# Attention, gated MLP and mixture on one core: products with V four tiles behind the scores, four buffers of transposed exponentials and two of split ones

## The chip, the cores and the metric

The program runs on one core of a Trainium2 chip. A core has five engines that each take their instructions in order from a queue of their own: TensorE (PE, with its weight loads shown apart as PEld), VectorE (DVE), ScalarE (ACT), GpSimd (POOL) and SyncE (SP), which here only issues transfers. They meet through semaphores. The metric is the device time of one execution in microseconds; what is compared is the median of several executions.

## The reference, cut to what matters

```
scores = scale * q @ k.T                      # 4 batches, 8 heads, 576 keys, head 64
thresh = max(scores, -1) - tau
scores = where(scores >= thresh, scores, -1e9)
attn   = exp(scores - max(scores));  attn /= sum(attn)
x      = (attn @ v), heads side by side       # 2304 tokens x 512
xn     = x / rms(x) * g
x      = (silu(xn @ w_gate) * (xn @ w_val)) @ w_out
P      = balance(exp(x @ w_gate2))            # 8 rounds of row and column sums
out    = sum over 8 experts e of P[:, e] * (relu(x @ w1[e]) @ w2[e])
```

The change lies in the attention, in the step from the exponentials to their product with V.

## The kernel before, in words

The program has two stages on one TensorE. In the first, attention and the gated MLP run together. In the second, the mixture of experts runs alone; nothing of the change touches it.

Attention goes by 144 tiles, one for 128 queries of one head (32 a batch), or for 64 remaining queries of two heads (4 a batch). For a tile, `att_tile` issues the following. TensorE computes the scores S (L282, four matmuls of 288 columns, eight in a tile of remaining queries) into one of two PSUM buffers. VectorE takes their maximum (L292). ScalarE makes two small tables (L293, L297) and the exponential e (L296), which VectorE masks by the threshold while it sums it (L298); this is the last reading of S, and it frees the PSUM buffer for the tile after the next. ScalarE then rounds e to 16 bits into the first half of a tile `hl` (L303), and GpSimd writes what the rounding left out into the second half (L304, L305). SyncE issues one transfer that transposes `hl` into a tile `eT` (L307). TensorE at last multiplies `eT` with V (L330, `att_values`, 14 matmuls of 64 columns, 28 in a tile of remaining queries).

Since that chain is long, the product with V of a tile isn't issued with its scores. A list `waiting` holds the tiles whose products are still open, and when it holds more than `LAG` of them, the oldest is issued behind the scores of the present tile, `with tc.issue_after(last.ins)`: on TensorE's queue it can't stand ahead of them. `LAG` also sets at which tile of a batch V is rounded (`prepare`, the calls of `prep_v`), and how many products follow after the last scores.

`hl` has three buffers and `eT` three. A buffer of `hl` can be written again when the transposing transfer of its earlier tile has landed; one of `eT` when the products of its earlier tile are done. The waits stand on ScalarE's queue (ahead of L303) and on SyncE's (ahead of L307).

When a group of tiles has ended (`end_main`, `end_rem`), its rows are scaled (L376, L395), normalised and sent transposed to the MLP. The gated MLP takes two groups at a time: `mlp_in` (L530 on TensorE, L538 to L545 on ScalarE, VectorE and GpSimd), then `mlp_out` (L561). Its weights are decoded and scaled during the first tiles.

The order on each queue is fixed before the program runs, by a planner with modelled durations: of what its plan has ready on an engine it takes the attention first (`attention_order`), and the MLP where attention isn't ready. On the chip an instruction that comes to the head of its queue too early holds everything behind it.

Of the kernel before, what the change touches and what calls it, by code (L numbers as in the profile page):

```python
# [8 lines left out]
F16 = mybir.dt.float16  # L9
# [10 lines left out]
def kernel(  # L20
# [25 lines left out]
    B, H, S, D = q.shape  # L46
# [3 lines left out]
    P = 128  # L50
# [92 lines left out]
    pa = pa_cm.__enter__()  # L143
# [91 lines left out]
    def prep_v(st, a):  # L235

        b, s_v = st["b"], st["s_v"]
        vs = pa.tile([P, 2, H2, NW, D], F16, tag="vs", name=f"vs{b}_{a}", bufs=2)
        st["vs"].append(vs)
        r = st["raw_v"][:, a * H2 : (a + 1) * H2]  # L240
        A.activation(vs[:, 0], r, AF.Copy, scale=s_v[:, 0:1])
        V.scalar_tensor_tensor(
            vs[:, 1].rearrange("p h c d -> p (h c d)"),
            r.rearrange("p h c d -> p (h c d)"),
            s_v[:, 0:1],
            vs[:, 0].rearrange("p h c d -> p (h c d)"),
            ALU.mult,
            ALU.subtract,
        )

    def prep_q(st, c):
        b = st["b"]
        qs = pa.tile([P, H, 2, D], F16, tag="ks", name=f"qs{b}_{c}", bufs=2)
        qr, s_q = st["raw_q"], st["s_q"]
        A.activation(qs[:, :, 0, :], qr[:, :, c, :], AF.Copy, scale=s_q[:, c : c + 1])
        V.scalar_tensor_tensor(
            qs[:, :, 1, :], qr[:, :, c, :], s_q[:, c : c + 1], qs[:, :, 0, :], ALU.mult, ALU.subtract
        )
        qT = pa.tile([P, H, P], F16, tag="qT", name=f"qT{b}_{c}", bufs=2)
        qX = pa.tile([P, H, P], F16, tag="qX", name=f"qX{b}_{c}", bufs=2)  # L260
        nc.sync.dma_start_transpose(out=qT, in_=qs.rearrange("p h l d -> p (h l d)"))
        nc.sync.dma_start(out=qX[0:64], in_=qT[64:128])
        nc.sync.dma_start(out=qX[64:128], in_=qT[0:64])
        st["q", c] = (qT, qX)
# [1 line left out]
    HS = S // 2  # L266

    waiting = []
    LAG = 3

    def att_tile(st, c, heads, slot, group):

        kT = st["kT"]
        qT, qX = st["q", c]
        nm = f"{st['b']}_{c}_{heads[0]}"
        sums = group["sums"]
        sp = psa.tile([P, 2, 512], F32, tag="S", name=f"S{nm}", bufs=2)
        rows = P // len(heads)
        for qq, first in ((qT, True), (qX, False)):
            for i, h in enumerate(heads):  # L280
                for j in range(2):
                    last = T.matmul(  # L282
                        sp[i * rows : (i + 1) * rows, j, 0:HS],
                        lhsT=qq[:, h, 0:rows],
                        rhs=kT[h // H2][:, h % H2, j * HS : (j + 1) * HS],
                        start=first,
                        stop=not first,
                    )
        sv = sp[:, :, 0:HS]
        nt = pa.tile([P, 3], F32, tag="nt", name=f"nt{nm}", bufs=4)  # L290
        mx = nt[:, 2:3]
        V.tensor_reduce(mx, sv, AX.XY, ALU.max)  # L292
        A.activation(nt[:, 0:1], mx, AF.Copy, scale=st["wt"][:, c : c + 1])  # L293
        e = pa.tile([P, S], F32, tag="e", name=f"e{nm}", bufs=3)
        ev = e.rearrange("p (a n) -> p a n", a=2)
        A.activation(ev, sv, AF.Exp, bias=nt[:, 0:1], scale=st["c2"][:, c : c + 1])  # L296
        A.activation(nt[:, 1:2], mx, AF.Identity, bias=st["bt"][:, c : c + 1])  # L297
        V.scalar_tensor_tensor(  # L298
            ev, sv, nt[:, 1:2], ev, ALU.is_ge, ALU.mult, accum_out=sums[:, slot : slot + 1]
        )  # L300

        hl = pa.tile([P, 2 * S], F16, tag="hl", name=f"hl{nm}", bufs=3)
        A.activation(hl[:, 0:S], e, AF.Copy)  # L303
        G.tensor_tensor(hl[:, S + REM :], e[:, 0 : NCH * P], hl[:, 0 : NCH * P], ALU.subtract)  # L304
        G.tensor_tensor(hl[:, S : S + REM], e[:, NCH * P :], hl[:, NCH * P : S], ALU.subtract)  # L305
        eT = pa.tile([P, 2 * S // P, P], F16, tag="eT", name=f"eT{nm}", bufs=3)
        nc.sync.dma_start_transpose(out=eT, in_=hl)  # L307
        waiting.append((st, heads, slot, group, eT))
        if len(waiting) > LAG:

            with tc.issue_after(last.ins):
                att_values(*waiting.pop(0))

    def att_values(st, heads, slot, group, eT):
        if slot == 0:
            group["pv"] = psa.tile([P, H * D], F32, tag="pv", name=f"pv{group['n']}", bufs=1)
        rows = P // len(heads)
        for i, h in enumerate(heads):
            vs, hh = st["vs"][h // H2], h % H2
            o = group["pv"][i * rows : (i + 1) * rows, slot * D : (slot + 1) * D]  # L320
            cols = slice(i * rows, (i + 1) * rows)
            mm = []
            for cc in range(NCH):
                mm.append((eT[:, cc, cols], vs[:, 0, hh, cc, :]))
                mm.append((eT[:, cc, cols], vs[:, 1, hh, cc, :]))
                mm.append((eT[:, NW + cc, cols], vs[:, 0, hh, cc, :]))
            mm.append((eT[:, NCH, cols], vs[:, 0, hh, NCH, :]))
            mm.append((eT[:, NCH, cols], vs[:, 1, hh, NCH, :]))
            for n, (a, r) in enumerate(mm):
                T.matmul(o, lhsT=a, rhs=r, start=n == 0, stop=n == len(mm) - 1)  # L330
        if slot == group["last"]:
            ended.append(group)
# [296 lines left out]
    def prepare(b, o):  # L629

        st = states[b]
        if o < NCH * H and o % H == 1:
            prep_q(st, o // H + 1)
        if b > 0 and o in (LAG - 3, LAG - 1):
            prep_v(st, (o - LAG + 3) // 2)
        if b + 1 == B:
# [33 lines left out]

    for t in range(len(row) + LAG):
        before = tc.cur_priority
        with attention_order():
            if t < len(row):
                b, c, heads, n, g = row[t]
                if n == 0:
                    g["sums"] = pa.tile([P, H], F32, tag="sums", name=f"sums{g['n']}", bufs=2)
                att_tile(states[b], c, heads, n, g)
                prepare(b, t % SLOTS)
            else:  # L680
                att_values(*waiting.pop(0))
            done = list(ended)
            ended.clear()
            for g in done:
                (end_main if g["c"] < NCH else end_rem)(g)
        first += tc.cur_priority - before
        for g in done:
            i = g["i"]
            if i == 1:
                for gi in range(NG):  # L690
                    prep_group(gi)
                first = tc.cur_priority
                tT = mlp_in(0)
                prep_out()
                mlp_out(0, tT)
            elif i is not None and i % 2 == 1 and i < len(tiles) - 1:
                mlp_out(i // 2, mlp_in(i // 2))
# [283 lines left out]
```

## Time and profile before

| what | us |
|---|---|
| median of 3 runs | 2198.3 (2198.22 to 2200.58) |
| the profiled execution | 2195.02 |
| its span, first to last instruction | 2193.2 |
| TensorE busy | 2032.0 |
| VectorE busy | 1490.2 |

The profile shows one execution. Engine shares are averages over both stages; the first tile of attention starts at about 39 us, the last product with V at 623 us, and the gated MLP ends at about 720 us. In the rows below, a gap before an instruction is given with what ended it: `[2.09 <-DMA eT<-hl]` means that the engine was idle for 2.09 us until the transfer from `hl` to `eT` had landed. `x14` counts instructions.

### The profile page before, as it was taken

To read this page: it belongs to the slowest core of one execution; us is meant where nothing else is said; L and a number is where in the kernel's file an instruction comes from. 1 tells how busy PE (TensorE), PEld (TensorE's weight loads), DVE (VectorE), ACT (ScalarE), POOL (GpSimd) and SP (SyncE) were. 2 spreads that over 40 slices of the span, in tenths; PEclk is the share of its full clock that TensorE was granted. 3 is DMA by queue.
4 is the path that set the end of the run, shared out by engine and by line. 5 is a ranking of instruction groups with operands and counts; after the bars stand their busy time and mean duration, and the time that the engine had idled before them with its cause. 6 is when DMAs were issued, how large, how long until landed. Compare 5 with 4: busy or idle time off the path is not lost.

```text
span 2193.2 us, 35334 instructions
## 1 busy us (share of the span) xinstructions
PE 2032.0 (93%) x13872; PEld 1194.7 (54%) x13872; DVE 1490.2 (68%) x3026; ACT 870.9 (40%) x1774; POOL 471.0 (21%) x572
## 2 busy tenths in 40 slices
PE   1358789899999999999999999999999999999999
PEld 0236667666876755545555555555555555555554
DVE  6999677777744287865775765766757757666554
ACT  6878778877843243311221221222212212222111
POOL 1347556665743231000000000000000000000000
PEclk9859999999999999999999999999999999999999
DMA  9895879867826051000100100100001001000001
GB/s 267 207 201 100 169 145 174 159 144 115 147 55 142 18 144 40 29 30 1 39 20 20 39 20 20 39 20 20 20 20 39 20 20 39 20 20 1 1 28 60
DMA packets 321879, 154.10 MB, mean 70 GB/s; under 512 B 278960, under 2 KB 292400, under 8 KB 321712
## 3 DMA queue, kind: packets, MB, share of 16 engines
q1 hardware_dynamic: 321120, 151.82, 30.4%
q8 instruction: 108, 1.77, 0.3%
q14 instruction: 59, 0.48, 0.1%
q0 software_dynamic: 64, 0.00, 0.0%
q10 hardware_dynamic: 528, 0.02, 0.0%
HBM read 68.18 MB, written 12.98 MB: 37 GB/s over the span
## 4 chain that ended last, share of the span: by engine, by line
PE 70%; DVE 2%; DMA 1%; SPq 1%; POOL 0%; issue 0%; ACT 0%; DVEq 0%; ACTq 0%
PE y L906 33%; PE h L860 28%; PE gv L530 5%; PE x L561 2%; PE pv L330 1%; DMA w1r<-in_moe_w_dram 1%; SPq L762 0%; PE S L282 0%; DMA x2T<-x2d 0%; DVE w L714 0%; DMA w2r<-in_moe_w_dram 0%; DMA eT<-hl 0%; PE logits L804 0%; DVE w1m L725 0%; POOL xh L601 0%
## 5 line engine op out<-in xcount | busy, mean ns | idle before, releaser
L860 PE MATMUL h<-x2T,w 128*128 128x384 f16 x4032 | 703.8, 326 | 9.9 <-DMA x2T<-x2d 3.9
L860 PEld LDWEIGHTS <-w 128*128 128x128 f16 x4032 | 394.1, 98 | 300.0 <-issue 14.2
L921 DVE SCALAR_TENSOR_TENSOR acc<-y,coef,acc 128x512 f32<-128x512 f32 x270 | 198.1, 746 | 283.0 <-PE y L906 282.9
L730 POOL TENSOR_TENSOR w1s<-w1r 128x512 f32<-128x512 f32 x16 | 20.3, 1271 | 1060.3 <-DMA w1r<-in_moe_w_dram 1006.3
L304 POOL TENSOR_TENSOR hl<-e,hl 128x512 f16<-128x512 f32 x144 | 172.8, 1200 | 228.2 <-ACT hl L303 146.2
L906 PE MATMUL y<-w,hD 128*128 128x512 f16 x864 | 219.9, 379 | 0.0
L906 PE MATMUL y<-w,hA 128*128 128x512 f16 x864 | 210.6, 379 | 0.9 <-DVE acc L921 0.6
L906 PE MATMUL y<-w,hC 128*128 128x512 f16 x864 | 210.0, 379 | 0.2 <-ACT acc L917 0.2
L906 PE MATMUL y<-w,hB 128*128 128x512 f16 x864 | 210.0, 379 | 0.0
L848 ACT ACTIVATE hA<-u 128x384 f16<-128x384 f32 x96 | 50.2, 522 | 341.1 <-DVE u L876 320.9
L848 ACT ACTIVATE hB<-u 128x384 f16<-128x384 f32 x96 | 50.2, 523 | 312.1 <-DVE u L880 311.2
L530 PE MATMUL gv<-xnT,wg 128*128 128x256 f16 x1296 | 167.8, 278 | 4.5 <-DVE u L540 3.0
L530 PE MATMUL gv<-xnT,wv 128*128 128x256 f16 x1296 | 167.5, 275 | 0.0
L330 PE MATMUL pv<-vs,eT 128*128 128x64 f16 (+1 forms) x2240 | 103.1, 201 | 50.3 <-DMA eT<-hl 47.3
L561 PE MATMUL x<-wo,tT 128*128 128x512 f16 x648 | 144.4, 379 | 1.0 <-DVE u L540 0.9
L906 PEld LDWEIGHTS <-hB 128*128 128x128 f16 x864 | 84.5, 98 | 101.9
L530 PEld LDWEIGHTS <-wg 128*128 128x128 f16 x1296 | 126.5, 100 | 24.0 <-issue 4.1
L298 DVE SCALAR_TENSOR_TENSOR e<-S,nt,e 128x576 f32<-128x576 f32 x144 | 116.3, 809 | 32.0 <-ACT e L296 31.5
L906 PEld LDWEIGHTS <-hD 128*128 128x128 f16 x864 | 84.6, 98 | 95.4
L530 PEld LDWEIGHTS <-wv 128*128 128x128 f16 x1296 | 126.4, 99 | 16.0 <-issue 0.2
L906 PEld LDWEIGHTS <-hC 128*128 128x128 f16 x864 | 84.7, 98 | 91.9 <-issue 0.3
L330 PEld LDWEIGHTS <-eT 128*128 128x128 f16 (+1 forms) x2240 | 91.0, 106 | 79.1 <-DMA eT<-hl 62.1
(244 smaller groups left out, 2852.1 us busy)
## 6 DMA issues: line engine op xcount, KB each, us to landing
w1r<-in_moe_w_dram SPq DMA_DIRECT2D x16, 1024.0 KB, 4.9
w2r<-in_moe_w_dram SPq DMA_DIRECT2D x16, 1024.0 KB, 5.3
wgatew<-in_moe_w_gate_dram SPq DMA_DIRECT2D x12, 512.0 KB, 6.0
wo<-in_moe_w_out_dram SPq DMA_DIRECT2D x12, 512.0 KB, 4.2
wvalw<-in_moe_w_val_dram SPq DMA_DIRECT2D x12, 512.0 KB, 4.5
x2d<-xs SPq DMA_DIRECT2D x24, 256.0 KB, 2.5
qX<-qT SPq DMA_DIRECT2D x40, 128.0 KB, 3.5
raw_k<-in_k_dram SPq DMA_DIRECT2D x4, 1024.0 KB, 6.2
```

The source lines that it names most:

```text
L298: V.scalar_tensor_tensor(ev, sv, nt[:, 1:2], ev, ALU.is_ge, ALU.mult, accum_out=sums[:, slot : slot + 1])
L304: G.tensor_tensor(hl[:, S + REM :], e[:, 0 : NCH * P], hl[:, 0 : NCH * P], ALU.subtract)
L330: T.matmul(o, lhsT=a, rhs=r, start=n == 0, stop=n == len(mm) - 1)
L530: T.matmul(gv[:, a, :], lhsT=w[:, l, kk, f * P : (f + 1) * P], rhs=xt[:, r * KD + kk, :], start=n == 0, stop=n == 3 * KD - 1,)
L561: T.matmul(ps, lhsT=tT[f][:, l, o : o + P], rhs=wo[:, f, r, :], start=n == 0, stop=n == 3 * KF - 1,)
L730: G.tensor_tensor(sm[:, 0], a21, a22, ALU.add)
L848: A.activation(t[:, 0, :], src, AF.Relu)
L860: T.matmul(ps, lhsT=w[:, a, l, kk, f * P : (f + 1) * P], rhs=xb[:, b * 4 + r * 2 + kk, :], start=n == 0, stop=n == 5,)
L906: T.matmul(ps, lhsT=hs[a][f][:, l, jj * P : (jj + 1) * P], rhs=w2[:, r, f, :], start=n == 0, stop=n == 3 * KH - 1,)
L921: V.scalar_tensor_tensor(acc[i], ps, coef[h][:, i : i + 1], acc[i], ALU.mult, ALU.add)
```

## The change

`LAG` becomes 4 in place of 3, so that a tile's products with V stand behind the scores of the fourth tile after it. `hl` has two buffers in place of three and `eT` four in place of three; a tile of either takes 2304 bytes a partition, so the memory stays the same. Through `LAG`, the two calls of `prep_v` for batches 1 to 3 move from tiles 0 and 2 of a batch to tiles 1 and 3, and four products instead of three follow the last scores.

```diff
     waiting = []
-    LAG = 3
+    LAG = 4
 
     def att_tile(st, c, heads, slot, group):
...
-        hl = pa.tile([P, 2 * S], F16, tag="hl", name=f"hl{nm}", bufs=3)
+        hl = pa.tile([P, 2 * S], F16, tag="hl", name=f"hl{nm}", bufs=2)
         A.activation(hl[:, 0:S], e, AF.Copy)
         G.tensor_tensor(hl[:, S + REM :], e[:, 0 : NCH * P], hl[:, 0 : NCH * P], ALU.subtract)
         G.tensor_tensor(hl[:, S : S + REM], e[:, NCH * P :], hl[:, NCH * P : S], ALU.subtract)
-        eT = pa.tile([P, 2 * S // P, P], F16, tag="eT", name=f"eT{nm}", bufs=3)
+        eT = pa.tile([P, 2 * S // P, P], F16, tag="eT", name=f"eT{nm}", bufs=4)
         nc.sync.dma_start_transpose(out=eT, in_=hl)
         waiting.append((st, heads, slot, group, eT))
         if len(waiting) > LAG:
```

## Rows read from the trace of the kernel before

**Rows 1.** The page: busy time, share of the span and instructions of each engine.
```profile
PE 2032.0 (93%) x13872; PEld 1194.7 (54%) x13872; DVE 1490.2 (68%) x3026; ACT 870.9 (40%) x1774; POOL 471.0 (21%) x572
```

**Rows 2.** Busy time by stretch: PE, PEld, DVE, ACT, POOL; then granted clock, DMA.
```profile
60.00:160.00 100.00, 44.95 (x370) 27.26 (x370) 95.03 (x197) 81.76 (x169) 40.21 (x42) 0.69 0.86 201
160.00:520.00 360.00, 320.65 (x3547) 244.48 (x3545) 276.88 (x658) 283.62 (x660) 222.19 (x293) 0.97 0.78 147
520.00:625.00 105.00, 103.98 (x1179) 77.39 (x1178) 73.75 (x176) 78.01 (x179) 71.30 (x99) 1.00 0.74 132
625.00:725.00 100.00, 95.93 (x709) 69.53 (x708) 34.67 (x80) 30.28 (x63) 30.09 (x38) 0.98 0.39 88
```

**Rows 3.** Waits of PE, 160 to 625 us: total, times, longest.
```profile
PE pv L330 <- DMA eT<-hl: 22.7, 21, 3.8
PE S L282 <- DVE e L298: 5.2, 5, 1.9
```

**Rows 4.** Waits of PE, 60 to 160 us.
```profile
PE pv L330 <- DMA eT<-hl: 24.6, 8, 4.7
PE S L282 <- DVE e L298: 19.1, 7, 6.9
```

**Rows 5.** Timeline of PE at two of the waits: start, us, instruction, idle before.
```profile
241.98 0.93 PE L330 MATMUL pv<-vs,eT 128*128 128x64 f16 x14 [3.76 <-DMA eT<-hl]
...
322.27 0.26 PE L330 MATMUL pv<-vs,eT 128*128 128x64 f16 x3 [2.27 <-DMA eT<-hl]
322.37 0.41 PE L282 MATMUL S<-kT,qT 128*128 128x288 f16 x2
322.62 0.41 PE L282 MATMUL S<-kT,qX 128*128 128x288 f16 x2
322.86 0.48 PE L330 MATMUL pv<-vs,eT 128*128 128x64 f16 x11
```

**Rows 6.** PE behind those waits: busy, granted clock, DMA share, GB/s.
```profile
242.00:246.00 4.00, 4.00 (x33) 0.59 0.94 247
324.00:332.00 8.00, 7.33 (x59) 0.59 0.51 97
```

**Rows 7.** Tile hl, 160 to 625 us: ns min/median/max, first and last start.
```profile
L303 ACT ACTIVATE hl<-e x122: 665/674/686, 161.8 to 614.1; 128x576 f16<-128x576 f32 x122
L304 POOL TENSOR_TENSOR hl<-e,hl x122: 1149/1158/1692, 162.6 to 614.9; 128x512 f16<-128x512 f32 x122
L305 POOL TENSOR_TENSOR hl<-e,hl x122: 297/308/1556, 163.7 to 616.0; 128x64 f16<-128x64 f32 x122
...
  DMA eT<-hl: 1.3, 2
...
DMA to landing us min/median/max: 3.2/3.4/7.1
```

**Rows 8.** The chain of waits, 546.9 to 558.5 us: start, us, what.
```profile
549.71 0.69 ACT hl L303
...
551.90 0.70 POOL x2t L589
...
552.83 4.97 DMA eT<-hl
```

**Rows 9.** Timeline of ACT in the same stretch.
```profile
555.77 0.67 ACT L303 ACTIVATE hl<-e 128x576 f16<-128x576 f32 x1
556.34 0.46 ACT L538 ACTIVATE u<-gv,g 128x256 f32<-128x256 f32 x1
556.70 0.29 ACT L293 ACTIVATE nt<-nt,wt 128x1 f32<-128x1 f32 x1
```

**Rows 10.** Timelines of DVE and PE: a mask, and the scores two tiles on.
```profile
561.07 0.82 DVE L298 SCALAR_TENSOR_TENSOR e<-S,nt,e 128x576 f32<-128x576 f32 x1 [0.89 <-ACT e L296]
...
563.21 0.41 PE L282 MATMUL S<-kT,qT 128*128 128x288 f16 x2
```

**Rows 11.** Tile hl, 520 to 625 us.
```profile
L303 ACT ACTIVATE hl<-e x31: 667/677/686, 522.5 to 614.1; 128x576 f16<-128x576 f32 x31
```

## The prediction

> **What bounds the kernel now.** I read the page first: TensorE is busy for 93% of the span, VectorE for 68% [rows 1]. The end is set by TensorE's work plus its idle time, so I asked for the engines by stretch, to see where that idle time lies. Up to 160 us VectorE is the bound (95.0 of 100 us busy, TensorE 45.0). From 160 to 520 us TensorE is busy for 320.7 of 360 us, so it idles 39 us; from 520 to 625 us it idles 1 us; behind that there is only MLP work until the mixture [rows 2]. The stretch that a change of the attention can win from is thus 160 to 520 us, and its price list is TensorE's waits: 22.7 us in 21 waits of L330 for the transfer from `hl` to `eT`, and 5.2 us in five waits of L282 for the mask of L298 [rows 3]. So the products with V do come too early on TensorE's queue; more than half of what can be won there is this wait. Before 160 us the same wait takes 24.6 us and the scores' wait 19.1 us [rows 4], while VectorE has hardly a pause.
>
> **The change, part by part.** *Products one tile later.* After 160 us, 122 tiles start between 161.8 and 614.1 us [rows 7], one every 452.3/121 = 3.74 us. A product that stands one tile later has 3.74 us more on average, as long as the longest wait (3.8 us). But tiles come in pairs on TensorE. At 241.98 us MLP matmuls follow the late product, and the whole 3.76 us can go; at 322.27 us the next scores follow at once, and the product is only pushed behind them (two rows of 0.41 us that overlap by 0.16, so 0.5 us up to the next group) and behind the products of the tile before (0.4 us): 0.9 us of cover [rows 5]. Of the 21 waits eleven are over 0.9 us. One is that at 241.98 us; I give 0.9 us to each of the other ten, though some have MLP matmuls between as well, and that leaves 5.8 us of their 14.8. Gain: 22.7 - 5.8, about 17 us. From both sides: 0 (all moves into another wait) and 22.7 us.
>
> *The clock.* Behind two of the waits the granted clock falls to a mean of 0.59, that is, to 1.2 of 2.4 GHz for most of these stretches: 4 us busy behind the wait of 3.76 us, and 7.33 us busy behind that of 2.27 us and a wait for scores [rows 6]. At full clock this work would be shorter by up to 0.41 x 11.3 = 4.6 us. The second stretch has its other wait left, so I take half: 2.3 us, between 0 and 4.6.
>
> *Two buffers of split exponentials.* This is the price. A buffer of `hl` is held from the start of L303 until the transfer has landed. At medians: ScalarE 0.67, GpSimd 1.16 + 0.31, landing 3.4 = 5.5 us [rows 7], and more where something stands in between: in the chain, L303 starts at 549.71, an MLP subtraction of GpSimd stands ahead of the issue, and the transfer lands at 557.80, 8.1 us later [rows 8]. L303 of two tiles on started at 555.77 [rows 9]; with two buffers it would wait for 2.0 us. With three, ScalarE waited for such a landing for 1.3 us in all [rows 7]. I set each of the 122 L303 against the landing of two tiles before (issue plus its own time to landing): 59 of them start before it, by 73.3 us in all, 4.8 us at most. Behind the waiting L303 on ScalarE's queue stand the Tanh of the MLP (L538) and the tables of the next tile (L293) [rows 9], behind those the exponential, the mask, and the scores of two tiles on. ScalarE is busy for 361.6 of 465 us between 160 and 625 (283.6 and 78.0 [rows 2]), so 73 us would fit into its idle 103 but use most of it. What reaches TensorE is what the scores have no slack for. At 563.21 us scores start 1.3 us after the mask of two tiles before has ended (561.07 + 0.82) [rows 10]; paired like this the median over the 122 tiles is 1.56 us. Of the 59 late starts 18 are late by more than 1.5 us, by 18.4 us beyond it. Part of this falls on moments where TensorE has products with V ready ahead of the scores, which now are a tile older. I take a little over half, 10 us. The ends are 0 (the planner spreads the tiles where it runs out of buffers) and 27 us (rival 1). I take a value nearer to the row-by-row sum than to either.
>
> The Trainium skill, on its page "Trainium Kernel Development and Optimization", section "Best Practices", asks for two buffers where a transfer is to overlap with compute. By that rule the third buffer was spare, the price would be 0, and the sum would come to some 2179 us. The trace bears that out only while a hold stays under two tiles' time; the hold of 8.1 us does not. I go by the rows.
>
> *Four buffers of transposed ones.* The issue of L307 now waits for the products of four tiles before, which themselves come one tile later: the same distance. Zero, with the same distance hiding it. *prep_v and the last products.* V of a batch is rounded one tile later and needed one tile later: zero. Its ScalarE and VectorE work meets other neighbours, which I bound by plus or minus 1 us. The last products end one tile later at most, with some 96 us of MLP matmuls left after 625 us [rows 2] that need none of them at first: zero; without that cover it would be one tile, 3.7 us.
>
> *Before 160 us.* VectorE idles 5 us of 100 [rows 2], so no more than 5 us can be won although TensorE's two waits there sum to 43.7 us [rows 4]. The missing buffer can cost as much. I take 0, between -5 and +5.
>
> The sum: -17 - 2.3 + 10 = -9 us on the profiled execution's own 2195.0 (its span of 2193.2 and 1.8 us around it), 2186 us. The median of the runs shown lies 3.3 us above that execution, which gives 2189 us.
>
> **The rivals.** *1. Two buffers set the pace: slower.* Held as long as in this trace (mean of the 122 pairs of start and landing: 6.96 us), two buffers pass one tile in 3.48 us. The mean pace is 3.74 us, but from 520 to 625 us the 31 tiles come every (614.1 - 522.5)/30 = 3.05 us [rows 11], and their mean hold of 6.68 us allows 3.34. TensorE is full there [rows 2], so 30 x 0.29 = 8.7 us would be new idle time; with the whole 18.4 us of the late starts it is 27 us, against a gain of 17: +10, 2208 us. It decides from the point at which holds exceed twice the planned tile time. For it: tiles come in pairs, holds of 8 us occur, and 18 of 122 tiles would start later than the scores have slack for. Against it: unhindered, the hold is 5.5 us, and the planner also sees that there are two buffers and can put MLP matmuls between.
>
> *2. One wait for another: no change.* Products stop waiting, and the scores of L282 wait instead for masks that come late: 17 us against 17 to 20, 2196 to 2200 us. For it: L282's wait already exists in five places. Against it: the slack of 1.56 us at the median.
>
> *3. The price is hidden: clearly faster.* All waits of L330 go, both stretches of low clock with them, and up to 3 of the 5 us before 160 us: 22.7 + 4.6 + 3 = 30 us, 2168 us. For it: ScalarE's idle 103 us. Against it: ten of the eleven long waits may have only 0.9 us of cover.
>
> That the change doesn't move the products is hardly possible, since `issue_after` ties them to the later scores; that the planner's order of everything else comes out different, with waits of its own of a few microseconds either way, is in all ranges.
>
> **How the numbers follow.** The forecast (a gain of 5 to 17 us, so 2181 to 2193 around 2189) has a chance of 0.42, rival 1 0.25, rival 2 0.17, rival 3 0.16. The predicted time is the forecast's, 2189 us. A measurement of this kernel can tell about 0.2%, 4.4 us, from no change. The forecast lies beyond it nearly all through (0.39 of its 0.42), rival 3 wholly: faster 0.55. Rival 2 and the edges of the forecast and of rival 1 give the same: 0.20. The rest of rival 1 is slower: 0.25. The range reaches from 2166 us (rival 3 and 2 us) to 2212 (rival 1 and 4 us).
>
> **What would show it.** Right: the wait of L330 for `eT` between 160 and 625 us falls from 22.7 to some 6 us; ScalarE gets a wait of L303 for the transfer, from 1.3 to some tens of microseconds; L282's wait for L298 grows by about 10 us; TensorE's idle time between 160 and 520 us falls from 39 to about 30. Wrong: L303 hardly waits (the price was none), or TensorE idles from 520 to 625 us as well and L282's wait grows by 20 us or more (rival 1), or L330 still waits for 15 us or more, since the pairs of tiles give it no more time.

## The result, and the profile after

The changed kernel takes 2211.2 us at the median against 2198.3 us of the kernel before run beside it: ratio 1.0051 (95% interval 1.0039 to 1.0064), 12.9 us slower. (Here and below the microseconds are differences of medians. The ratio is formed over the runs otherwise than as the quotient of the two medians, which is 1.0059 here; it is given for its interval.) The forecast was 2189 us; the time is near that of rival 1, which had 2208.

The page of the kernel after, its span and its busy times (before: [rows 1]):

```profile
span 2210.5 us, 35361 instructions
PE 2038.1 (92%) x13872; PEld 1195.8 (54%) x13872; DVE 1496.6 (68%) x3026; ACT 870.5 (39%) x1774; POOL 471.6 (21%) x572
```

The span grew by 17.3 us (this profiled execution is 1.2 us above the median, that of before 3.3 below). TensorE has the same 13872 matmuls; it is busy 6.1 us longer, and so idle 11.2 us longer. The same stretches as in [rows 2], and the piece in which its clock differs most (busy time of PE, PEld, DVE, ACT, POOL, then granted clock and DMA):

```profile
60.00:160.00 100.00, 41.50 (x355) 26.23 (x354) 92.25 (x189) 79.50 (x162) 39.87 (x40) 0.64 0.84 195
160.00:520.00 360.00, 318.21 (x3416) 239.00 (x3416) 271.37 (x642) 274.55 (x640) 214.27 (x285) 0.96 0.78 144
520.00:625.00 105.00, 99.46 (x1084) 73.19 (x1082) 75.33 (x169) 77.09 (x179) 65.92 (x91) 1.00 0.70 125
...
160.00:240.00 80.00, 63.48 (x642) 47.29 (x642) 65.60 (x151) 55.85 (x135) 47.40 (x57) 0.87 0.64 122
```

Idle time of TensorE: 58.5 us from 60 to 160 (before 55.0), 41.8 from 160 to 520 (39.4), 5.5 from 520 to 625 (1.0). So the loss is in every stretch of the attention, and the full stage of before, 520 to 625 us, now has gaps. From 160 to 240 us the granted clock is 0.87 at the mean (before 0.98); from 190 to 196 and from 220 to 226 us TensorE was busy for 2.6 and 0.7 of 6 us, and in the 6 us behind each the clock is 0.60 and 0.54, that is, at the lower of its two levels (1.2 of 2.4 GHz) for most of them. By an estimate this makes TensorE's work from 160 to 240 us longer by 0.11 x 63.5 = 7 us in this execution.

Waits of TensorE and of ScalarE from 160 to 640 us, which takes in the later end of the attention (before, up to 625 us: [rows 3]; ScalarE's wait for the landing was 1.3 us [rows 7]):

```profile
PE pv L330 <- DMA eT<-hl: 16.5, 24, 1.7
PE S L282 <- DVE e L298: 11.9, 11, 3.4
PE x L561 <- DVE u L540: 6.8, 1, 6.8
PE gv L530 <- DVE u L540: 4.4, 6, 1.9
...
ACT hl L303 <- DMA eT<-hl: 47.0, 46, 2.7
```

The products with V do wait less (22.7 to 16.5 us), but scores wait for masks 6.7 us more, and the last row is new: ScalarE stands still 46 times, 47 us in all, until a transfer has freed one of the two buffers of `hl`. What that looks like on ScalarE's queue (timeline: start, us, instruction, idle before):

```profile
505.51 0.68 ACT L303 ACTIVATE hl<-e 128x576 f16<-128x576 f32 x1 [1.17 <-DMA eT<-hl]
506.10 0.40 ACT L544 ACTIVATE tT<-u 128x256 f16<-128x256 f32 x1
508.22 0.68 ACT L303 ACTIVATE hl<-e 128x576 f16<-128x576 f32 x1 [1.72 <-DMA eT<-hl]
508.81 0.49 ACT L224 ACTIVATE ks<-raw_k,k_s 128x256 f16<-128x256 f32 x1
509.21 0.28 ACT L293 ACTIVATE nt<-nt,wt 128x1 f32<-128x1 f32 x1
```

Behind the waiting L303 stand the MLP (L544), the keys of the next batch (L224) and the tables of the next tile (L293). The tile `hl` over the same stretch (ns min/median/max, first and last start; before: [rows 7]):

```profile
L303 ACT ACTIVATE hl<-e x123: 666/682/686, 162.9 to 639.6; 128x576 f16<-128x576 f32 x123
...
  DMA eT<-hl: 47.0, 46
...
DMA to landing us min/median/max: 3.2/3.4/7.3
```

L303 takes 682 ns at the median, before 674; the tiles follow one another every (639.6 - 162.9)/122 = 3.91 us in place of 3.74, and the last L303 starts at 639.6 us in place of 614.1. Set against the landing of two tiles before, 60 of these 123 L303 start within 0.13 us behind it (three in the trace of before): half of the tiles run at the limit of the ring.

### The profile page after: what moved, and what is told of

Same layout as the page of the kernel before. It is cut to its first block, busy times and chain, and to the rows that moved or that the text cites. A ratio compares the mean times of both kernels' runs of the same rounds, so it can differ in the third digit from the quotient of the medians.

```text
span 2210.5 us, 35361 instructions
## 1 busy us (share of the span) xinstructions
PE 2038.1 (92%) x13872; PEld 1195.8 (54%) x13872; DVE 1496.6 (68%) x3026; ACT 870.5 (39%) x1774; POOL 471.6 (21%) x572
## 4 chain that ended last, share of the span: by engine, by line
PE 67%; DVE 2%; DMA 1%; issue 0%; POOL 0%; SPq 0%; ACT 0%; DVEq 0%; POOLq 0%; ACTq 0%
PE y L906 33%; PE h L860 28%; PE gv L530 4%; PE x L561 2%; DMA w2r<-in_moe_w_dram 1%; DMA x2T<-x2d 0%; DVE w L714 0%; DMA w1r<-in_moe_w_dram 0%; SPq L762 0%; DMA eT<-hl 0%; DVE w1m L725 0%; PE logits L804 0%; PE pv L330 0%; POOL xh L601 0%; DVE hB L849 0%
## 5 line engine op out<-in xcount | busy, mean ns | idle before, releaser
L561 PE MATMUL x<-wo,tT 128*128 128x512 f16 x648 | 145.8, 383 | 6.8 <-DVE u L540 6.8
L906 PEld LDWEIGHTS <-hA 128*128 128x128 f16 x864 | 84.4, 98 | 90.3 <-issue 2.3
L282 PE MATMUL S<-kT,qT 128*128 128x288 f16 (+1 forms) x320 | 65.7, 312 | 67.9 <-DVE e L298 49.2
```

The lines of the kernel that those rows point to most:

```text
L282: last = T.matmul(sp[i * rows : (i + 1) * rows, j, 0:HS], lhsT=qq[:, h, 0:rows], rhs=kT[h // H2][:, h % H2, j * HS : (j + 1) * HS], start= ...
L561: T.matmul(ps, lhsT=tT[f][:, l, o : o + P], rhs=wo[:, f, r, :], start=n == 0, stop=n == 3 * KF - 1,)
L906: T.matmul(ps, lhsT=hs[a][f][:, l, jj * P : (jj + 1) * P], rhs=w2[:, r, f, :], start=n == 0, stop=n == 3 * KH - 1,)
```

## The experiments

Theories: A, the missing buffer of `hl` is the loss; B, the later products are; C, the planner's new layout is, by chance, whatever the edit; D, the planner spreads tiles because there are two buffers, however long they are held. All edits are to the kernel before unless the text says otherwise; all ratios are against runs of the kernel before on the same chip.

**e1, two buffers of hl alone.**
```diff
-        hl = pa.tile([P, 2 * S], F16, tag="hl", name=f"hl{nm}", bufs=3)
+        hl = pa.tile([P, 2 * S], F16, tag="hl", name=f"hl{nm}", bufs=2)
```


> One part alone: two buffers of split exponentials, products still three tiles behind, three buffers of transposed ones. Theory A (the missing hl buffer is the loss): 2205 to 2220 us, slower than the whole change or equal to it, since the products haven't moved; ScalarE's L303 waits for the landed transfer for 30 to 60 us between 160 and 640 us, and L330 waits for at least the 22.7 us of before. Theory B (the products one tile later are the loss: groups end later, the MLP's matmuls come later): 2196 to 2200 us. Theory C (any edit makes the planner lay out the queues anew, by chance this much worse): no relation to the buffers, anywhere from 2190 to 2212.

Measured: 2213.9 us, ratio 1.0069 (1.0051 to 1.0087), 15.7 us slower, as A has it. Waits from 160 to 640 us:

```profile
PE pv L330 <- DMA eT<-hl: 27.5, 27, 3.5
PE gv L530 <- DVE u L540: 7.5, 8, 2.5
PE S L282 <- DVE e L298: 3.9, 4, 1.8
...
ACT hl L303 <- DMA eT<-hl: 45.1, 41, 3.5
```

ScalarE's wait is there without the rest of the change. TensorE waits more at the products (27.5 us) and at the MLP (7.5 us for `u`, before 3.0), since nothing has moved the products. Its same matmuls also keep it busy for 6.3 us longer than before (2038.3 us), as in the whole change.

**e2, the products alone.** Three buffers of each.
```diff
-    LAG = 3
+    LAG = 4
```


> The other part alone: products four tiles behind, three buffers of hl and three of eT. Theory A: 2185 to 2198 us; L303 waits for under 3 us, L330 for under 10 us; the transfers of L307 wait longer for a buffer of eT, which is what is late next. Theory B: 2205 to 2215 us. Theory C: anywhere from 2190 to 2212.

Measured: 2195.2 us, ratio 0.9987 (0.9978 to 0.9996): 3.0 us faster. The two parts add up: 15.7 - 3.0 = 12.7, and the whole change has 12.9. B falls. One expectation was missed: L303 waits for a landing for 8.6 us with all three buffers, where I had under 3. Waits of TensorE from 160 to 640 us:

```profile
PE S L282 <- DVE e L298: 12.2, 8, 3.2
PE pv L330 <- DMA eT<-hl: 8.8, 13, 2.0
PE gv L530 <- DVE u L540: 6.2, 7, 1.5
PE gv L530 <- ACT x2f L581: 4.8, 3, 2.5
```

The wait of L330 fell by 13.9 us, more than in the full change. But L282 rose by 7.0, the MLP's wait for `u` by 3.2, and one for `x2f` is new with 4.8. All waits of TensorE in this stretch sum to 37.3 us, before to 39.8 and in the whole change to 47.5.

**e3, the change with three buffers of hl, paid by e.**
```diff
-    LAG = 3
+    LAG = 4
-        e = pa.tile([P, S], F32, tag="e", name=f"e{nm}", bufs=3)
+        e = pa.tile([P, S], F32, tag="e", name=f"e{nm}", bufs=2)
-        eT = pa.tile([P, 2 * S // P, P], F16, tag="eT", name=f"eT{nm}", bufs=3)
+        eT = pa.tile([P, 2 * S // P, P], F16, tag="eT", name=f"eT{nm}", bufs=4)
```


> The change with the third hl buffer given back; the memory comes from the tile e, which has two buffers in place of three. Theory A: 2178 to 2195 us if two buffers of e (held by exponential, mask, rounding and the two subtractions, some 4 to 5 us) suffice, with L303 waiting for under 3 us and L330 for under 8. If e is held too long, ScalarE's L296 waits for L305 of two tiles before and the time is over 2200. Theory B: 2205 to 2215. Theory C: 2190 to 2212.

Measured: 2197.9 us, ratio 0.9997 (0.9985 to 1.0008). The loss is gone, and nothing is gained. ScalarE waits for a landing for 2.8 us; scores wait for masks for 16.5 us. A tile `e` is held by engines alone, with no transfer in it, and two buffers carry it. A's range missed the time: its upper end (2195) was too low, and L330 still waits for 10.3 us where I had under 8.

**e4, a control of the planner.** `prep_v` one tile later, as the change has it.
```diff
-        if b > 0 and o in (LAG - 3, LAG - 1):
-            prep_v(st, (o - LAG + 3) // 2)
+        if b > 0 and o in (LAG - 2, LAG):
+            prep_v(st, (o - LAG + 2) // 2)
```


> A control: the kernel before with prep_v one tile later in each batch (as the change has it) and nothing else. Theories A and B: within 0.2% of before, 2194 to 2202 us. Theory C: it may lie anywhere from 2190 to 2212, since the planner lays out all queues anew.

Measured: 2198.9 us, ratio 1.0004 (0.9991 to 1.0017). This new layout isn't worth 13 us, and e2, e3, e12 and e15, each with a layout of its own, lie within 3.5 us of before as well; that any edit costs so much (C) falls. That an edit elsewhere can cost as much, e10 shows.

**e5 and e6, a shorter hold.** GpSimd's two subtractions become one memset, so the rounding rest of the exponentials is left out of the result; e5 has three buffers of `hl`, e6 two.
```diff
-        G.tensor_tensor(hl[:, S + REM :], e[:, 0 : NCH * P], hl[:, 0 : NCH * P], ALU.subtract)
-        G.tensor_tensor(hl[:, S : S + REM], e[:, NCH * P :], hl[:, NCH * P : S], ALU.subtract)
+        G.memset(hl[:, S:], 0.0)
```


> The base of a pair: the kernel before, with GpSimd's two subtractions for the second half of hl (1.16 and 0.31 us) replaced by one memset, so that the exponentials' rounding rest is left out of the product. This shortens the hold of a buffer of hl and takes work off GpSimd. Both theories: 2185 to 2199 us; by itself it tells only what the lighter GpSimd is worth.

> The same with two buffers of hl. Theory A (the price of the missing buffer comes from the hold being longer than two tiles' time): a hold of some 4.3 to 4.8 us in place of 5.5 and more lets two buffers pass a tile in 2.4 us, under the 3.05 us of the fastest stretch; the difference to e5 is 0 to 6 us, and L303 waits for the transfer for under 20 us, where e1 had 45. Theory D (the planner spreads the tiles because there are two buffers, whatever the hold): the difference to e5 is as large as e1's 15 us.

Measured: e5 2196.0 us, 0.9991 (0.998 to 1.0001); e6 2193.5 us, 0.9978 (0.9965 to 0.9991). Taking the buffer costs nothing here (e6 has 2.5 us less than e5), where it cost 15.7 us in e1, so D, by which two buffers cost whatever else holds, falls. Tile `hl` of e6 from 160 to 640 us:

```profile
L304 POOL MEMSET hl<- x121: 570/577/855, 163.2 to 612.0; 128x576 f16 x121
L303 ACT ACTIVATE hl<-e x121: 665/681/693, 165.5 to 612.0; 128x576 f16<-128x576 f32 x121
...
  DMA eT<-hl: 196.1, 112
...
  POOL hl L304: 181.9, 94
...
  ACT hl L303: 14.2, 18
```

From L303 to the landing the mean is 5.44 us (6.65 in e1, by the same pairing; I had expected 4.3 to 4.8). But the pair doesn't show what I meant it to: the memset needs no exponential, so it stands ahead of L303 and waits for the buffer in its place, 94 times on GpSimd, and L303 only 18 times. Counted from its first write, the memset, a buffer is held for 7.27 us at the mean, longer than in e1, so the length of the hold alone isn't what costs. A shorter way from L303 to the landing and another place of the wait act together.

**e7, one buffer of hl.** The change with `bufs=1`.

> Products four tiles behind, four buffers of eT and one of hl: the dose raised. Theory A: one buffer passes one tile a hold, so from the first L303 to the last lie at least 143 x 5.5 = 790 us (before: 565), up to 143 x 6.9 = 990; ScalarE waits for the landed transfer in nearly every tile; the attention ends at 840 to 1050 us, one pair of groups of the MLP behind it, and the time is 2310 to 2500 us. Theory D, with the wait on the queue of no account: the same stretch, but hardly any wait of L303, since the planner puts other work ahead.

Measured: 2403.1 us (one execution). Tile `hl` over the whole span:

```profile
L303 ACT ACTIVATE hl<-e x144: 666/683/687, 49.4 to 905.5; 128x576 f16<-128x576 f32 x144
...
  DMA eT<-hl: 199.7, 122
```

The tiles come every (905.5 - 49.4)/143 = 5.99 us: one hold (5.75 us at the mean from 160 us on) and a little. The ring sets the pace, as computed beforehand, and L303 waits in 122 of 144 tiles.

**e8, the change with three buffers of hl and e untouched.** The memory came from the tiles `xn` and `x2t`.
```diff
-        xn = pa.tile([P, 2, DM], F16, tag="xn", name=f"xn{i}", bufs=1)
+        xn = pa.tile([P, H, 2, D], F16, tag="ks", name=f"xn{i}", bufs=2)
...
-            wd = words(bits[f * P : (f + 1) * P, :], f"wo{f}", ("x2", "x2t")[f % 2])
+            wd = words(bits[f * P : (f + 1) * P, :], f"wo{f}", ("x2", "tT")[f % 2])
```


> Products four tiles behind with three buffers of hl, four of eT and three of e. The 2304 bytes come from elsewhere: xn takes its buffer from the ring ks, which has the same size, and every second word tile of w_out comes from the ring tT, so that x2t has three quarters. Theory A: at or below e2 (2195 us), 2186 to 2197, with L307 waiting less for products than in e2 (16.5 us), and L330 for eT for under 9 us. If xn and the rounded keys get into each other's way, ScalarE waits at L346 for a landed transfer, and the time is 2197 to 2205.

Measured: 2221.9 us, ratio 1.0114 (1.0098 to 1.0131), outside both. The trace shows a wait that has nothing to do with `hl`: TensorE waits once for the maximum of `w_out`, whose words now share a ring with the MLP. The move of `xn`, which costs something too (e10), is in this time as well, so e8 says nothing of the third buffer.

```profile
PE womxp L131 <- DVE om L500: 31.1, 1, 31.1
```

**e9 and e10, the same with other memory, and its control.** `xn` as in e8; `lg`, a tile of the mixture, moves to a later pool, `w_out` stays. e10 has LAG 3 and three buffers each.
```diff
-    lg = small([P, NTL, E], "lg")
...
+    lg = pc.tile([P, NTL, E], F32, tag="lg", name="lg")
```


> The change with the third hl buffer given back and nothing of w_out touched (in e8 TensorE waited once for 31.1 us for the maximum of w_out, om, since its words had lost a buffer, so e8 does not answer): xn takes its buffer from the ring ks, and the tile lg of the mixture moves to a pool that is opened after the attention. Theory A: the 12.9 us of the change go and some of the hoped gain appears, 2186 to 2197 us, L303 waiting for under 10 us, L330 for under 9. If a fourth eT buffer were what costs, it stays over 2205.

> The control of e9: the kernel before with the same two moves of memory (xn in the ring ks, lg in the later pool), LAG 3, three buffers each. Expected within 0.2% of before, 2194 to 2202; if xn in the ring ks costs or gains, e9 is to be read against this run.

Measured: e9 2208.3 us, 1.0043 (1.0029 to 1.0057); e10 2210.9 us, 1.0055 (1.004 to 1.007). e10 lies outside what I expected, and e9 where I had put it for the case that a fourth buffer of `eT` costs. The control was needed: the two moves of memory cost 12.5 us by themselves, so e9 can't be read against before. Against e10 it is 2.6 us faster, about what e2 gained with three buffers of `eT`; a fourth shows no worth of its own. L303 waits for 11.7 us in e9.

**e11 and e12, the rounding behind the next exponential.** e11 is the change, e12 has LAG 4 and three buffers each; in both L303 of a tile stands behind L296 of the next.
```diff
-        A.activation(ev, sv, AF.Exp, bias=nt[:, 0:1], scale=st["c2"][:, c : c + 1])
+        ex = A.activation(ev, sv, AF.Exp, bias=nt[:, 0:1], scale=st["c2"][:, c : c + 1])
...
+        if pending:
+            att_round(ex, *pending.pop(0))
+        pending.append((st, heads, slot, group, e, nm))
...
+            with tc.issue_after(ex.ins):
+                A.activation(hl[:, 0:S], e, AF.Copy)
```


> The change, with the rounding L303 of a tile put behind the exponential of the next tile on ScalarE's queue, so that a waiting L303 no longer holds that exponential; products still four tiles behind, two buffers of hl, four of eT. If the price is what stands behind the waiting L303 (exponential, mask, scores), it falls by more than half: 2196 to 2204 us. If the price is the ring itself (two buffers, hold of 5.5 to 7 us), it stays: 2207 to 2220, and L303 still waits for over 30 us.

> The control of e11 with three buffers of hl and three of eT, products four tiles behind, L303 behind the next exponential: near e2, 2190 to 2200 us, since there is hardly a wait of L303 to go round; the transposing starts a tile later, so L330 may wait more for eT than e2's 8.8 us after 160 us, and the time can be up to 2206.

Measured: e11 2214.6 us, 1.0072 (1.0057 to 1.0087); e12 2195.0 us, 0.9985 (0.9974 to 0.9996). The price of the buffer, 19.6 us from e12 to e11, stays though the next exponential stands ahead. (The two differ in `eT` as well, whose fourth buffer showed no worth in e9.) ScalarE's wait for the landing in e11, and TensorE's for the products in e12, both from 160 to 640 us:

```profile
ACT hl L318 <- DMA eT<-hl: 44.3, 38, 4.0
```
```profile
PE pv L341 <- DMA eT<-hl: 21.3, 18, 2.3
PE S L282 <- DVE e L298: 2.1, 5, 0.7
```

So the price doesn't need the way by which I had it reach TensorE (that one exponential late, its mask, its scores); what stays is the ring of two. A waiting L303 still holds the exponentials after that one, so the queue as a way isn't excluded. And e12 is as fast as e2 with more than twice its wait at L330; all waits of TensorE sum to 37.2 us there, in e2 to 37.3.

**e13, two tiles behind.** `LAG = 2`, `prep_v` at tiles 0 and 1. Theory F: a wait of L330 costs its length; G: TensorE's waits replace one another.

> Products two tiles behind in place of three (prep_v at tiles 0 and 1 of a batch), three buffers each: the dose of LAG the other way. Theory F (a wait of L330 taken away is worth its length to TensorE): L330 waits for 40 us or more between 160 and 640 us and the time grows by about as much as the wait, 2213 to 2240. Theory G (the waits of TensorE between 160 and 520 us replace one another, since scores, products and MLP all hang on the same chain of attention tiles): the time grows by less than half of what the wait grows.

Measured: 2200.5 us, ratio 1.0017 (1.0003 to 1.003), 2.9 us slower. TensorE's waits from 160 to 640 us, and the stretches 160 to 520 and 520 to 625 us:

```profile
PE pv L330 <- DMA eT<-hl: 30.2, 29, 3.8
PE gv L530 <- DVE u L540: 6.5, 5, 2.4
PE gv L530 <- ACT x2f L581: 4.8, 1, 4.8
```
```profile
160.00:520.00 360.00, 317.23 (x3526) 242.24 (x3524) 279.99 (x660) 286.37 (x664) 224.10 (x294) 0.97 0.77 148
520.00:625.00 105.00, 99.96 (x1124) 73.31 (x1121) 71.76 (x167) 76.37 (x174) 66.54 (x93) 1.00 0.74 129
```

The wait of L330 grew by 7.5 us, where theory F had 17 and more, and the median by 2.9. By these two numbers G would be the better, but they aren't of the same executions: the profiled one of e13 lies 3.9 us above its median, that of before 3.3 us below, and between the two the span grew by 9.4 us and all waits of TensorE by 7.5 (39.8 to 47.3). Here nothing took another wait's place, so e13 doesn't decide between F and G. What speaks for G is e2 and e12.

**e14 and e15, the MLP's subtraction on VectorE.** e14 is the change, e15 is e2, each with:
```diff
-            G.tensor_tensor(t[:, 1, :], u, t[:, 0, :], ALU.subtract)
+            V.tensor_tensor(t[:, 1, :], u, t[:, 0, :], ALU.subtract)
```


> The change, with the MLP's subtraction L545 (0.67 us on GpSimd, ahead of which or behind which L304 and the issue of L307 often stand) moved to VectorE. Nothing is left out. If the price is the hold, it gets shorter without the MLP's work on GpSimd, L303 waits for under 35 us in place of 47, and the time falls below the change's, 2198 to 2208 us, unless VectorE, which then has some 45 us more work between 160 and 640, becomes late for the masks (over 2212).

> The control of e14: e2 (products four tiles behind, three buffers each) with L545 on VectorE. If VectorE has room for it, 2190 to 2198 us, and the difference e14 - e15 is the price of the buffer with the shorter hold, under 12 us; if not, over 2200.

Measured: e14 2220.4 us, 1.011 (1.0089 to 1.013); e15 2197.8 us, 0.9995 (0.9983 to 1.0007). The hold didn't get shorter (6.82 us at the mean, 6.80 in the change), so the edit doesn't test what it was for. It does give another price of the buffer, 22.5 us from e15 to e14, where I had expected under 12 (here too `eT` differs as in e11 and e12). VectorE is late for the MLP in both, so that this alone isn't what makes e14 slow (from 160 to 640 us, e14, then e15):

```profile
PE gv L530 <- DVE u L540: 17.3, 9, 6.4
...
ACT hl L303 <- DMA eT<-hl: 35.5, 37, 2.8
```
```profile
PE gv L530 <- DVE u L540: 16.3, 11, 4.5
...
ACT hl L303 <- DMA eT<-hl: 4.5, 3, 2.7
```

## Why the prediction was wrong

*What bounds the kernel.* The reading of the stage held: the loss lies where TensorE had its gaps. The waits of L330 are real, and the change takes some of them. What was wrong is their worth.

*The step that failed: "Gain: 22.7 - 5.8, about 17 us".* Alone (e2), the products one tile later are worth 3.0 us. The subtraction of 5.8 us was near: L330 kept 8.8 us in e2. But I set each microsecond of this wait equal to one of the end, and wrote the possibility that another wait takes its place only as rival 2. In e2 this wait is 13.9 us shorter and all waits of TensorE together 2.5; e12 has 21.3 us of this wait at e2's time. Scores, masks, products and MLP blocks hang on the same tiles, and in e2 the engine that no longer stands at the products stands at the masks and the MLP (15.0 us more). In the changed kernel itself L330 kept 16.5 us, more than the 15 that I had named as a sign of being wrong; the pairs of tiles, my reason for that sign, aren't it, since e2 with its third buffer of `hl` keeps 8.8.

*The clock.* Its 2.3 us can't be told apart within e2's 3.0. TensorE's busy time, with the same matmuls, is 2.6 us shorter in e2 than before, near that term, but 6.1 us longer in the kernel after and 6.3 in e1: the missing buffer seems to cost clock as well, for which the sum had no term. These are single executions, and e12 has 3.0 us more without a loss.

*The second term: "a little over half, 10 us", for two buffers of hl.* The mechanism was right and its sign too; the price is 15.7 us (e1), 15.9 (e2 to the change), 19.6 (e12 to e11) and 22.5 (e15 to e14). Two things in the working speak for why it was too small. I took only what exceeded the scores' slack of 1.5 us, as if each late tile stood alone; but a late L303 makes its landing late, and so L303 of two tiles on: in the kernel after, half of the tiles run at the ring's limit and the last starts 25.5 us later. And I counted on slack on the path to the scores, while e11 shows that the price doesn't hang on the next exponential alone. The 73.3 us of late starts became 47.0 us of waits of L303, since the tiles moved apart.

*Rival 1* had the mechanism, the place (ScalarE at L303, gaps from 520 to 625 us: 4.5 us more than before, where 8.7 were computed) and nearly the time, 2208 for 2211.2. Its price of 27 us was too high and its gain of 17 too, and the two errors met: that its time came so near is luck. The rule that I quoted from the Trainium skill ("Trainium Kernel Development and Optimization", "Best Practices": two buffers to overlap a transfer with compute) would have had the third buffer spare; e1 measures it at 15.7 us here, and e6 shows two enough where L303 to the landing is 5.4 us and the wait stands on GpSimd.

*Four buffers of eT* at zero: no run shows a worth (e9 against e10 gains 2.6 us, e2 without it 3.0). *prep_v* at zero within 1 us: e4, +0.6 us. *Before 160 us* at zero between -5 and +5: L330's wait there fell from 24.6 to 0.6 us and L282's rose from 19.1 to 37.3, while VectorE stayed the bound; the first MLP matmul starts at 162.0 us in place of 156.7, and at 160.8 in e2 and 161.3 in e1, so each part alone shows most of that delay, and e2 is faster all the same. *The last products* at zero: the gated MLP's last matmuls (L561) end at 772 us in the trace of before, not at about 720, so the work left behind them was more than the 96 us.

Open is how much of the price is ScalarE standing still, and how much the planner's own spreading of tiles, since it plans with the same two buffers; no kernel here parted the two. A count in the traces speaks against spreading as the whole of it: ahead of the start of its last L303, TensorE has begun 2152 of the 3240 MLP matmuls in e1, and 2150 before, so e1 pays its 15.7 us with the tiles set no further apart in work, while the change (2224, e2 2184) and e11 (2256, e12 2129) do have more MLP between their tiles. That e6 lost nothing may be due to the shorter way from L303 to the landing or to the wait's place on GpSimd; e7 shows that a ring at its limit sets the pace by its hold, and no run shows the other's part.

The fastest version that leaves nothing out is e2 (with e12 beside it): LAG 4 with three buffers each, 0.9987 of before.

## What to carry to other kernels

Before a buffer is taken from a ring, set the hold, from the write that the others wait for to the landing of the transfer that reads it, against buffers times the pace, and let a delay run on through the ring. Here a hold of 6.8 us was already too long for two buffers: that is nine tenths of two tiles at the mean pace before (7.5 us) and more than two tiles in the fastest stretch (6.1 us). An early first write on an engine off the path (the memset of e6) makes the hold longer and needn't cost. One wait of the bounding engine isn't what its removal gives: 13.9 us less of it gave 3.0 in e2, and 1.4 us less gave 3.4 in e12. The sum of all its waits went the way of the time in all of these (2.5 us less in e2, 2.6 less in e12, 7.7 more in the change); look for what else depends on the same chain, and price it by a run with that edit alone. Where memory for an experiment is borrowed, run the loan by itself first.

## What the runs showed that I had not expected

Letting `xn` share the two-buffer ring of the rounded keys and queries, together with the move of `lg`, costs 12.5 us (e10), with no single wait that would explain it: from 160 to 640 us L330 waits as before (23.3 us), L282 for 14.2 us in place of 5.2, and L303, with all its three buffers, for 12.7 us in place of 1.3. It is again a ring of two whose buffers are held by a transposing transfer, and L346, which writes `xn`, waits there for the landing of `kT` for 5.7 us; that this sharing and not the move of `lg` is the cause isn't shown. And the time from the issue of the transposing transfer of `hl` to its landing hardly differs: 3.2 us at the least and 3.4 at the median in the kernel before and in the one after, 3.2 and 3.2 with a single buffer (e7); what varies is its tail, up to 7.3 us in the kernel after and 8.6 in e1, and the work ahead of its issue.
